# Batch 0 of an attention and gated MLP kernel: k'v partly in fp32, the first weight columns by casting loads

## The chip, the cores and the metric

The kernel runs on one core of one Trainium2 chip, in one launch. The metric is the time of one execution on the device in microseconds (us), of which the median over the runs is given.

Engines are named as in the profile: PE is TensorE (PEld its weight loads), DVE VectorE, ACT ScalarE, POOL GpSimd, SP SyncE. SP and ACT issue plain loads and stores; POOL issues the loads that convert fp32 to fp16 on the way ("casting loads").

## The reference

Linear attention without a softmax, a root-mean-square norm over each head, and a gated MLP behind it:

```python
q, k, v: (batch 8, heads 8, tokens 576, 64) fp32
kv  = einsum('bhsd,bhse->bhde', k, v)          # 64x64 per head
out = einsum('bhsd,bhde->bhse', q, kv)
x   = out / sqrt(mean(out*out, -1) + 1e-6) * g_norm
x   = x.transpose(0, 2, 1, 3).reshape(4608, 512)
ffn = (gelu(x @ w_gate) * (x @ w_val)) @ w_out  # d_ff 1536
y   = x + sigmoid(x @ w_res) * ffn              # (4608, 512) fp32
```

## The kernel before

**Tiling.** A batch has 576 tokens: 512 go through as a block of 128 partitions by NJ = 4 tokens each, and the 64 left ("the last tokens") of all batches make a ninth block at the end. For k'v all 576 tokens count, so in each batch the last 64 tokens are added to the sum. Heads go in four pairs (`pr`), because two heads of 64 fill 128 columns. The MLP's 1536 hidden columns are 12 blocks of 128 (`f`); the gate and value weights lie in four chunks of columns, of 256, 256, 512 and 512 (`WCS`), so chunk 0 is needed for blocks 0 and 1, chunk 1 for 2 and 3, and so on.

**Batch 0, "the opening".** Nothing can overlap the first batch's attention, so it is cut into pieces by pair, and these are issued in an order written out by hand: the string `opening` (L1335 to L1340). Each word is a piece, its digit the pair, and a last letter A, D or P says which engine does it (ACT, DVE, POOL). `f_piece` (L1288) turns words into instructions. Every engine works off its own instructions strictly in the order of the string. The words, in the order in which a pair needs them:

- `qc`, `kc`, `vc`: q, k, v of the pair cast from the loaded fp32 to fp16 (L1175, L1177)
- `lk`, `lv`: the last tokens of half of the heads (two pairs), cast and spread. They arrive as 32 rows of two tokens for each of four heads, row by row interleaved; `lk` multiplies k by a 0/1 column per head (`of_head`), so that a full 128-row product picks the right head (L1186), `lv` makes two copies of v (L1195)
- `qT`, `qo`: q transposed on PE, copied out of PSUM (L1203, L1206)
- `kv`: k'v of the pair in PSUM, four matmuls over the 512 tokens (L1214), two for the last tokens (L1220); `kvo`: copied out by DVE times a mask that clears the blocks between different heads (L1223)
- `o`: q (k'v) (L1228); `sq`, `rd`, `rt`, `ri`: square on ACT, sum on DVE, root on ACT, reciprocal on DVE; `t`: o times that, on DVE (L1253)
- `xT`, `xo`: t transposed on PE, copied out with a scaling by g_norm, on DVE or ACT (L1269, L1271). The fourth pair goes in two halves, a and b, from `sq` on
- `g`, `v`: the pair's share of the gate and value products of hidden blocks 0 and 1 (L1280)
- `warm`: matmuls on zeros with no use but to keep PE busy; `gelu`: the load of ACT's table for gelu
- `wcg`, `wcv`: chunk 0 of the weights cast from its fp32 load, half a chunk each (L1307); `wg`, `wv`: POOL issues the casting load of a chunk (L156)

Behind the opening PE goes on with hidden blocks 2 to 7 (`m_gval`, L443), a group for blocks 8 to 11 (L981), the residual gate (L464) and the output product (`fps`, L481), into which batch 1's attention is mixed.

**Loads.** SP issues first: q, k, v of batch 0 as fp32 (two pairs at once, then pair by pair, with the last tokens in between), then chunk 0 of both weights as fp32 in four loads (L1118). All other weights, and batch 1 from 19.5 us on, come by casting loads from POOL's queue, in the order of the opening and behind it: wg1, wv1, wg2, wv2, wg3, wv3, wr, q, k, wo, v, and so on.

Of the kernel before, what the change touches and what calls it, by code (L numbers as in the profile page):

```python
# [18 lines left out]
def kernel(  # L19
# [55 lines left out]
    pmoe, pattn = Banks(3, 1, 0, 2, opening=(0,)), Banks(4, 5, 6, 7)  # L75
# [15 lines left out]
    raw, b16_t, qr_t = {}, {}, {}  # L91
# [49 lines left out]
    wg_c, wv_c = [], []  # L141
# [58 lines left out]
    def halves(e):  # L200
        return slice(e * D, (e + 1) * D)
# [863 lines left out]

    tiles_16(0)
    raw[0, "q"] = wo_ts.bitcast(FP32)[:, 0 : H * NJ * D].rearrange("p (h x) -> p h x", h=H)
    hid_of = {}
    for which in "kv":
        if which == "k":  # L1070
            t = hidp.tile([P, NF, NJ * P], FP16, tag="hid", name=which + "f").rearrange("p a b -> p (a b)")
        else:
            t = hid_s
        hid_of[which] = t
        raw[0, which] = t.bitcast(FP32)[:, 0 : H * NJ * D].rearrange("p (h x) -> p h x", h=H)

    def load_first(which, t, lo, hi):
        nc.sync.dma_start(out=raw[0, which][:, lo:hi, :], in_=rows4(t, 0, lo, hi))


    first_raw, first_last = [], []
    for which in "kv":
        t = hid_of[which]
        rest = t[:, 2 * H * NJ * D :]
        if which == "k":
            first_last.append(rest[:, 0 : 2 * H * D].rearrange("p (j h d) -> p j h d", j=2, h=H))
        else:
            first_last.append(rest[:, 0 : 8 * D].rearrange("p (i j e d) -> p i j e d", i=2, j=2, e=2))
        first_raw.append([th_all[:, 2 * len(first_raw) + i, 0 : 2 * D] for i in range(2)])

    def load_first_last(half):
        hs = slice(half * HH, (half + 1) * HH)
        for i, t in enumerate((k, v)):
            nc.sync.dma_start(
                out=first_raw[i][half],
                in_=t[0, hs, M0:S, :].rearrange("h (p j) d -> p h (j d)", j=2),
            )

    grow = consts.tile([1, D], FP32, name="grow")
# [5 lines left out]
    for pr in range(NP // 2, NP):  # L1105
# [2 lines left out]
        if pr == NP // 2:  # L1108
            load_first_last(1)
        load_first("v", v, 2 * pr, 2 * pr + 2)  # L1110
    w_raw = {}
    for n, t in (("g", moe_w_gate), ("v", moe_w_val)):
        pool, tag = (stage, "qraw") if n == "g" else (qkvp, "k16")
        w_raw[n] = pool.tile([P, H, NJ * D], FP16, tag=tag, name=f"w{n}f")
        w_raw[n] = w_raw[n].rearrange("p a b -> p (a b)").bitcast(FP32).rearrange("p (c f) -> p c f", c=NP)
    for cs in (slice(0, NP // 2), slice(NP // 2, NP)):
        for n, t in (("g", moe_w_gate), ("v", moe_w_val)):
            nc.sync.dma_start(  # L1118
                out=w_raw[n][:, cs, :], in_=t[:, 0 : WCS[0]].rearrange("(cc p) f -> p cc f", p=P)[:, cs, :]
            )  # L1120
    ident32 = moep.tile([P, P], FP32, tag="ge", name="ident32")
    make_identity(nc, ident32)

# [11 lines left out]
    nc.vector.memset(one32, 1.0)  # L1135
    ident = consts.tile([P, P], FP16, name="ident")
    nc.vector.tensor_copy(out=ident, in_=ident32)
    of_head = consts.tile([P, HH], FP32, name="of_head")
    nc.vector.tensor_reduce(
        out=of_head, in_=ident32.rearrange("p (r h) -> p h r", h=HH), op=ALU.add, axis=mybir.AxisListType.X  # L1140
    )
    grow32 = moep.tile([1, 2, D], FP32, tag="ge", name="grow32")
    nc.vector.tensor_copy(out=grow32, in_=grow[:, None, :].to_broadcast([1, 2, D]))
    grow16 = moep.tile([1, H, D], FP16, tag="ge", name="grow16")
# [15 lines left out]
    xT0, t0 = xT_t[0], t_t[0]  # L1160
    rms0 = consts.tile([P, NJ, H], FP32, name="rms0")
    rinv0 = consts.tile([P, NJ, H], FP32, name="rinv0")
    first = {}

    tiles = {}
    engines = {"A": nc.scalar.copy, "D": nc.vector.tensor_copy, "P": nc.gpsimd.tensor_copy}

    def of_pair(pr):
        return slice(2 * pr, 2 * pr + 2), slice(pr * P, (pr + 1) * P)

    def f_cast(which, pr, copy):
        hs, _ = of_pair(pr)
        dst, src = b16_t[0, which], raw[0, which]
        if which == "v":
            copy(out=dst[:, hs, :], in_=src[:, hs, :])  # L1175
        else:
            copy(  # L1177
                out=dst.rearrange("p j h d -> p h j d")[:, hs, :, :],
                in_=src.rearrange("p h (j d) -> p h j d", j=NJ)[:, hs, :, :],
            )  # L1180

    def f_k_last(half, engs):

        raw_ = first_raw[0][half].rearrange("p (j d) -> p j d", j=2)
        for j, eng in enumerate(engs):
            eng.tensor_tensor(  # L1186
                out=first_last[0][:, j, half * HH : (half + 1) * HH, :],
                in0=raw_[:, j, None, :].to_broadcast([P, HH, D]),
                in1=of_head[:, :, None].to_broadcast([P, HH, D]),
                op=ALU.mult,  # L1190
            )

    def f_v_last(half, copy):
        raw_ = first_raw[1][half].rearrange("p (j d) -> p j d", j=2)
        copy(out=first_last[1][:, half], in_=raw_[:, :, None, :].to_broadcast([P, 2, 2, D]))  # L1195

    BANK = {"qT": (6, 4, 7, 7), "kv": (7, 5, 6, 4), "o": (2, 1, 6, 4), "xT": (7, 5, 7, 4), "xTb": (0, 0, 0, 5)}

    def f_qT(pr):
# [5 lines left out]
    def f_qT_out(pr, copy):  # L1205
        copy(out=s0["qT"][:, :, pr, :], in_=first["qT", pr])  # L1206

    def f_kv(pr):

        first["kv", pr] = ps = pattn.tile([P, P], FP32, name="kvp", bank=BANK["kv"][pr])  # L1210
        k16 = b16_t[0, "k"].rearrange("p j h d -> p j (h d)")
        hs, cs = of_pair(pr)
        for j in range(NJ):
            nc.tensor.matmul(  # L1214
                ps, lhsT=k16[:, j, cs], rhs=b16_t[0, "v"][:, hs, j * D : (j + 1) * D], start=(j == 0), stop=False
            )
        for j in range(2):
            kl = first_last[0][:, j].rearrange("p h d -> p (h d)")[:, cs]
            vl = first_last[1][:, pr // 2, j].rearrange("p e d -> p (e d)")
            nc.tensor.matmul(ps, lhsT=kl, rhs=vl, start=False, stop=(j == 1))  # L1220

    def f_kv_out(pr):
        nc.vector.tensor_tensor(out=s0["kv2"][:, pr, :], in0=first["kv", pr], in1=mask, op=ALU.mult)  # L1223
# [64 lines left out]
    def f_piece(word):  # L1288

        name = word.rstrip("0123abADP")  # L1290
        rest = word[len(name) :]
        pr = int(rest[0])
        j0, j1 = {"a": (0, NJ // 2), "b": (NJ // 2, NJ)}.get(rest[1:2], (0, NJ))
        eng = rest[-1:]
        if name in ("qc", "kc", "vc"):
            f_cast(name[0], pr, engines[eng])
        elif name == "lk":
            f_k_last(pr, (nc.gpsimd if eng == "P" else nc.vector, nc.vector))
        elif name == "lv":
            f_v_last(pr, engines[eng])  # L1300
        elif name == "warm":
            keep_warm(pr)
        elif name in ("wg", "wv"):
            (load_wg if name == "wg" else load_wv)(pr, {"a": 0, "b": 1}.get(rest[1:2]))
        elif name in ("wcg", "wcv"):
            cs = slice(2 * pr, 2 * pr + 2)
            engines[eng](out=(wg_c if name == "wcg" else wv_c)[0][:, cs, :], in_=w_raw[name[-1]][:, cs, :])  # L1307
        elif name == "qo":
            f_qT_out(pr, engines[eng])
        elif name in ("qT", "kv", "kvo", "o", "rt", "ri"):  # L1310
            {"qT": f_qT, "kv": f_kv, "kvo": f_kv_out, "o": f_o, "rt": f_sqrt, "ri": f_rinv}[name](pr)
        elif name in ("sq", "rd", "t", "xT"):
            {"sq": f_sq, "rd": f_red, "t": f_t, "xT": f_xT}[name](pr, j0, j1)
        elif name == "xo":
            f_xT_out(pr, j0, j1, eng)
        elif name == "g":
            f_mm(wg_c, 0, pr, j0, j1)
        elif name == "v":
            f_mm(wv_c, 1, pr, j0, j1)
# [3 lines left out]
    gcol = consts.tile([P, 1], FP32, name="gcol")  # L1323
    g16 = consts.tile([P, C], FP16, name="g16")
# [8 lines left out]
    keep_warm(4)  # L1333

    opening = """  # L1335
    qc0A qc1D g16 qT1 qT0 kc0A kc1D lk0P qo1A qo0D lv0P warm3 vc1D gcol vc0P kv1 qc2A kv0 kvo1 o1 kvo0 kc2P qT2 o0
    lk1D sq1 lv1P warm3 sq0 rd1 vc2P rd0 rt1 kv2 qc3P qo2A warm2 ri1 kvo2 rt0 wg1 t1 kc3A o2 qT3 sq2 ri0 xT1 warm2 vc3P t0
    qo3A wv1 rd2 kv3 wcg0A xT0 warm1 kvo3 rt2 xo1D wcv0P o3 xo0A ri2 g1 t2 wg2 sq3b v1 sq3a rd3b wcg1A xT2 wv2a rd3a g0 xo2D
    rt3 v0 wv2b wcv1A ri3 g2 t3b wg3 t3a xT3b v2 xo3bD xT3a wv3 g3b xo3aD gelu v3b g3a v3a
    """  # L1340
    pattn.turn = [6, 7, 5, 4]

# [167 lines left out]
    for blk in GROUPS:  # L1510
        t = token_sums(blk, nc.vector)
# [49 lines left out]
    for blk in range(B + 1):  # L1561
# [130 lines left out]
```

## Time and profile before

| | us |
|---|---|
| median of three runs | 320.05 |
| the three runs | 327.7, 319.15, 320.05 |
| the profiled execution, its own time | 318.52 |
| its span, first to last instruction | 316.5 |
| mean granted TensorE clock in it | 0.995 of full |
| PE / DVE / ACT / POOL busy | 308.2 / 275.7 / 217.0 / 187.4 |

The page of the profile gives busy time for each engine, and the same in 40 slices of the span (7.9 us each, a digit for tenths). A line of the timeline has start and duration in us, the engine, the line of the program, the operation, the output and its inputs with their shapes, and how many instructions are merged in it. A line on DMA issues has target and source, the queue, how many, their size as they land, and the us from issue to landing. Windows give the busy time of each engine, the DMA engines' share and GB/s of each stretch.

### The profile page before, as it was taken

What the parts mean: (1) busy time and instruction counts of PE and PEld (TensorE: products, weight loads), DVE (VectorE), ACT (ScalarE), POOL (GpSimd) and SP (SyncE); (2) the same over time, 40 slices, a digit from 0 to 9 for tenths busy, and PEclk for the clock granted to TensorE, in tenths of its full rate; (3) what the DMA queues carried; (4) which work ended last, traced back from release to release, by engine and by line L of the source; (5) the groups of instructions that cost most, each with busy time, mean ns of one, the idle gap of its engine ahead of it and who ended that gap; (6) DMA issues with size and microseconds to landing.
All of it is one profiled execution on the core that took longest, in us unless ns stands there. A gap on an engine that the chain in (4) does not pass through costs nothing.

```text
span 316.5 us, 7841 instructions
## 1 busy us (share of the span) xinstructions
PE 308.2 (97%) x3071; PEld 249.1 (79%) x3071; DVE 275.7 (87%) x489; ACT 217.0 (69%) x395; POOL 187.4 (59%) x239
## 2 busy tenths in 40 slices
PE   7899999999999999999999999999999999999993
PEld 3555756844888888888888888888888888888882
DVE  5897998989898899989998999899998777897774
ACT  4764688685958794879487948795667367736760
POOL 2883352360799579856985798408850474396332
PEclk9999999999999999999999999999999999999997
DMA  7999999899969598389936994700630003001104
GB/s 253 330 201 204 200 198 197 154 171 209 121 78 177 180 158 110 72 198 150 116 67 201 128 124 71 217 4 0 78 142 1 2 5 131 0 2 59 76 2 133
DMA packets 77398, 38.91 MB, mean 123 GB/s; under 512 B 42290, under 2 KB 75058, under 8 KB 77362
## 3 DMA queue, kind: packets, MB, share of 16 engines
q0 software_dynamic: 39296, 17.17, 43.3%
q1 hardware_dynamic: 37488, 20.71, 26.1%
q8 instruction: 24, 0.39, 0.5%
q10 hardware_dynamic: 578, 0.52, 0.5%
q14 instruction: 12, 0.10, 0.1%
HBM read 38.80 MB, written 9.44 MB: 152 GB/s over the span
## 4 chain that ended last, share of the span: by engine, by line
PE 59%; DVE 1%; issue 0%; DVEq 0%
PE Av L981 10%; PE Ag L981 10%; PE wA L549 8%; PE Fv L981 5%; PE Fg L981 5%; PE rA L600 3%; PE w L549 2%; PE Eg L981 2%; PE Ev L981 2%; PE wF L549 2%; PE wE L549 2%; PE wD L549 2%; PE rF L600 2%; PE rE L600 1%; PE kvp L218 1%; PE op L240 1%
## 5 line engine op out<-in xcount | busy, mean ns | idle before, releaser
L1018 POOL TENSOR_TENSOR hid<-ge,c 128x512 f16<-128x512 f16 x23 | 26.8, 1165 | 36.5 <-ACT ge L1012 36.5
L549 PEld LDWEIGHTS <-hid_s 128*128 128x128 f16 x384 | 37.5, 98 | 4.5
L981 PEld LDWEIGHTS <-wsv 128*128 128x128 f16 x368 | 35.6, 98 | 4.8 <-issue 0.2
L981 PEld LDWEIGHTS <-wsg 128*128 128x128 f16 x368 | 35.8, 98 | 4.2
L394 POOL TENSOR_TENSOR t<-t,g 128x512 f16<-128x512 f16 x32 | 37.8, 1210 | 0.0
L737 POOL TENSOR_TENSOR osb<-osb,t 128x512 f32<-128x512 f32 x28 | 34.0, 1244 | 0.0
L991 ACT COPY Eg<-Ag 128x512 f32<-128x512 f32 x23 | 13.4, 582 | 26.2 <-PE Ag L981 25.6
L549 PEld LDWEIGHTS <-hid 128*128 128x128 f16 x288 | 28.1, 98 | 3.3
L981 PEld LDWEIGHTS <-wg 128*128 128x128 f16 x276 | 27.0, 98 | 3.6
L981 PEld LDWEIGHTS <-wv 128*128 128x128 f16 x276 | 27.0, 98 | 3.1
L981 PE MATMUL Ag<-ts,wsg 128*128 128x256 f16 x184 | 27.6, 273 | 0.0
L981 PE MATMUL Av<-ts,wsv 128*128 128x256 f16 x184 | 27.6, 272 | 0.0
L1002 DVE TENSOR_TENSOR Fg<-Ag,d 128x512 f32<-128x512 f32 x23 | 16.0, 696 | 12.0 <-ACT d L995 9.1
L268 DVE TENSOR_REDUCE ss<-sq 128x8 f32<-128x512 f32 x32 | 20.3, 677 | 0.6 <-ACT sq L263 0.5
L549 PE MATMUL wA<-wo_ts,hid_s 128*128 128x256 f16 x168 | 20.6, 272 | 0.0
L1012 ACT ACTIVATE ge<-Eg 128x512 f16<-128x512 f32 x23 | 13.7, 597 | 9.7 <-PE Eg L981 9.7
L1012 ACT ACTIVATE ge<-c 128x512 f16<-128x512 f32 x23 | 14.4, 625 | 8.0 <-DVE c L1002 8.0
L1012 ACT ACTIVATE ge<-Fg 128x512 f16<-128x512 f32 x23 | 13.6, 591 | 8.8 <-PE Fg L981 7.0
L1002 DVE TENSOR_TENSOR c<-Ag,d 128x512 f32<-128x512 f32 x23 | 15.8, 688 | 4.2 <-PE Ag L981 4.2
L377 DVE TENSOR_TENSOR t<-op,ny 128x512 f16<-128x512 f32 x28 | 18.7, 683 | 0.9 <-POOL ny L334 0.4
L1018 DVE TENSOR_TENSOR hid<-ge,Fv 128x512 f16<-128x512 f16 x23 | 15.6, 680 | 1.5 <-ACT kv L295 1.5
L1012 ACT ACTIVATE ge<-Ag 128x512 f16<-128x512 f32 x23 | 13.7, 598 | 4.1 <-PE Ag L981 4.0
(228 smaller groups left out, 857.1 us busy)
## 6 DMA issues: line engine op xcount, KB each, us to landing
out_dram<-osb SPq DMA_DIRECT2D x14, 512.0 KB, 3.6
qraw<-in_q_dram POOLq DMA_DIRECT2D x7, 512.0 KB, 6.4
k<-in_k_dram POOLq DMA_DIRECT2D x7, 512.0 KB, 7.9
v<-in_v_dram POOLq DMA_DIRECT2D x7, 512.0 KB, 10.7
wo<-in_moe_w_out_dram POOLq DMA_DIRECT2D x3, 384.0 KB, 11.9
wg<-in_moe_w_gate_dram POOLq DMA_DIRECT2D x2, 512.0 KB, 8.4
out_dram<-osb SPq DMA_DIRECT2D x4, 256.0 KB, 5.0
wv<-in_moe_w_val_dram POOLq DMA_DIRECT2D x3, 256.0 KB, 7.5
```

The costliest lines, as they stand in the source:

```text
L218: nc.tensor.matmul(ps[halves(e), pr, :], lhsT=k16[:, h, j * D : (j + 1) * D] if j < NJ else kl[:, h, :], rhs=v16[:, h, j * D : (j + 1) * D ...
L268: nc.vector.tensor_reduce(out=out_, in_=sqs.pop((b, i)), op=ALU.add, axis=mybir.AxisListType.X)
L377: nc.vector.tensor_tensor(out=t, in0=o, in1=scale, op=ALU.mult)
L394: eng.tensor_tensor(out=t_t[blk][:, jj, :], in0=t_t[blk][:, jj, :], in1=g16, op=ALU.mult)
L549: nc.tensor.matmul(ps[:, e - es[0], :], lhsT=a[:, f, e * P : (e + 1) * P], rhs=b[:, f, :], start=(start and e == es[0] and f == 0), stop=( ...
L600: nc.tensor.matmul(out_[:, e, :], lhsT=x_[:, e, cc, :], rhs=w_[:, cc, :], start=(first and e == 0 and cc == 0), stop=(cc == 1), skip_group ...
L737: nc.gpsimd.tensor_tensor(out=res_all[of], in0=res_all[of], in1=t_t[blk][of], op=ALU.add)
L981: nc.tensor.matmul(out_[:, r, :], lhsT=lhsT, rhs=rhs, start=(first and r == 0 and c == 0), stop=(c == 1), skip_group_check=True,)
L991: nc.scalar.copy(out=tile_of("E", u), in_=ps["A", u])
L1002: nc.vector.tensor_tensor(out=dst, in0=ps["A", u], in1=sb["d", u], op=ALU.add)
L1012: nc.scalar.activation(out=ge[q], in_=source(q, "g"), func=AF.Gelu)
L1018: eng.tensor_tensor(out=dst, in0=ge[q], in1=source(q, "v"), op=ALU.mult)
```

## The change

Only batch 0 is touched.

1. The last tokens are loaded with a head's 32 rows next to one another. `lk`, `lv`, `of_head` and the spread copies go. A new word `kl` multiplies the raw fp32 rows of a head on a corner of the array (32 rows by 64 columns, placed by `tile_position`) into the pair's diagonal block, as the first part of the sum; `kv` adds the 512 tokens to it. `kl` needs two products per head, fp32.
2. The third pair (pr = 2) is not cast: its k'v over the 512 tokens is made of eight fp32 matmuls (four j, two halves of 64 columns), straight from the loaded data. `kc2` and `vc2` go.
3. Chunk 0 of both weights comes by a casting load from POOL's queue (`wg0`, `wv0`, ahead of `wg1`, `wv1`); its four fp32 loads on SP and its casts `wcg`, `wcv` go.
4. `xo2` and the second half of `xo3` move from DVE to ACT; `qc3` goes from POOL to ACT, `kc3` from ACT to POOL. The order of the string changes with it: `t1` stands before `kvo2`, `xo1D` before `kvo3`, `g0` before `v1`, and there are 8 warm matmuls instead of 11.

```diff
             nc.sync.dma_start(
                 out=first_raw[i][half],
-                in_=t[0, hs, M0:S, :].rearrange("h (p j) d -> p h (j d)", j=2),
+                in_=t[0, hs, M0:S, :].rearrange("h (p j) d -> h p (j d)", j=2),
             )
...
-    for cs in (slice(0, NP // 2), slice(NP // 2, NP)):
-        for n, t in (("g", moe_w_gate), ("v", moe_w_val)):
-            nc.sync.dma_start(
-                out=w_raw[n][:, cs, :], in_=t[:, 0 : WCS[0]].rearrange("(cc p) f -> p cc f", p=P)[:, cs, :]
-            )
...
-    of_head = consts.tile([P, HH], FP32, name="of_head")
-    nc.vector.tensor_reduce(
-        out=of_head, in_=ident32.rearrange("p (r h) -> p h r", h=HH), op=ALU.add, axis=mybir.AxisListType.X
-    )
...
+    CAST = (0, 1, 3)
...
+    def f_kl(pr):
+
+        first["kv", pr] = ps = pattn.tile([P, P], FP32, name="kvp", bank=BANK["kv"][pr])
+        for j in range(2):
+            for e in range(2):
+                rows = slice((2 * (pr % 2) + e) * (P // HH), (2 * (pr % 2) + e + 1) * (P // HH))
+                kl, vl = (first_raw[i][pr // 2][rows, j * D : (j + 1) * D] for i in range(2))
+                nc.tensor.matmul(
+                    ps[halves(e), halves(e)],
+                    lhsT=kl,
+                    rhs=vl,
+                    start=(j == 0),
+                    stop=False,
+                    skip_group_check=True,
+                    tile_position=(rows.start, e * D),
+                )
+
     def f_kv(pr):
 
-        first["kv", pr] = ps = pattn.tile([P, P], FP32, name="kvp", bank=BANK["kv"][pr])
+        ps = first["kv", pr]
...
-        for j in range(2):
-            kl = first_last[0][:, j].rearrange("p h d -> p (h d)")[:, cs]
-            vl = first_last[1][:, pr // 2, j].rearrange("p e d -> p (e d)")
-            nc.tensor.matmul(ps, lhsT=kl, rhs=vl, start=False, stop=(j == 1))
+            if pr in CAST:
...
+                continue
+            for e in range(2):
+                nc.tensor.matmul(
+                    ps[halves(e), :],
+                    lhsT=raw[0, "k"][:, 2 * pr + e, j * D : (j + 1) * D],
+                    rhs=raw[0, "v"][:, hs, j * D : (j + 1) * D],
+                    start=False,
+                    stop=(j == NJ - 1),
+                    skip_group_check=True,
+                )
...
-    qc0A qc1D g16 qT1 qT0 kc0A kc1D lk0P qo1A qo0D lv0P warm3 vc1D gcol vc0P kv1 qc2A kv0 kvo1 o1 kvo0 kc2P qT2 o0
-    lk1D sq1 lv1P warm3 sq0 rd1 vc2P rd0 rt1 kv2 qc3P qo2A warm2 ri1 kvo2 rt0 wg1 t1 kc3A o2 qT3 sq2 ri0 xT1 warm2 vc3P t0
-    qo3A wv1 rd2 kv3 wcg0A xT0 warm1 kvo3 rt2 xo1D wcv0P o3 xo0A ri2 g1 t2 wg2 sq3b v1 sq3a rd3b wcg1A xT2 wv2a rd3a g0 xo2D
-    rt3 v0 wv2b wcv1A ri3 g2 t3b wg3 t3a xT3b v2 xo3bD xT3a wv3 g3b xo3aD gelu v3b g3a v3a
+    qc0A qc1D g16 qT1 qT0 kc0A kc1D qo1A qo0D kl1 kl0 warm2 vc1D gcol vc0P kv1 qc2A kv0 kvo1 o1 kvo0 wg0 qT2 o0
+    sq1 wv0 kl2 kl3 warm2 sq0 rd1 wg1 rd0 rt1 kv2 wv1 qo2A warm1 ri1 qc3A t1 kvo2 rt0 kc3P o2 qT3 sq2 ri0 xT1 warm2 vc3P t0
+    qo3A rd2 kv3 xT0 warm1 xo1D kvo3 rt2 o3 xo0A ri2 g1 t2 wg2 sq3b g0 sq3a rd3b xT2 wv2a rd3a v1 xo2A
+    rt3 v0 wv2b ri3 g2 t3b wg3 t3a xT3b v2 xo3bD xT3a wv3 g3b xo3aA gelu v3b g3a v3a
```

More of the change, by code (lines that the diff above doesn't have):

```diff
@@ L1067 @@
     raw[0, "q"] = wo_ts.bitcast(FP32)[:, 0 : H * NJ * D].rearrange("p (h x) -> p h x", h=H)
-    hid_of = {}
     for which in "kv":
@@ L1073 @@
             t = hid_s
-        hid_of[which] = t
         raw[0, which] = t.bitcast(FP32)[:, 0 : H * NJ * D].rearrange("p (h x) -> p h x", h=H)
@@ L1078, in load_first @@
         nc.sync.dma_start(out=raw[0, which][:, lo:hi, :], in_=rows4(t, 0, lo, hi))
-    first_raw, first_last = [], []
+    first_raw = []
     for which in "kv":
[L1083 to L1088, printed above, removed]
         first_raw.append([th_all[:, 2 * len(first_raw) + i, 0 : 2 * D] for i in range(2)])
@@ L1110 @@
         load_first("v", v, 2 * pr, 2 * pr + 2)
-    w_raw = {}
-    for n, t in (("g", moe_w_gate), ("v", moe_w_val)):
-        pool, tag = (stage, "qraw") if n == "g" else (qkvp, "k16")
-        w_raw[n] = pool.tile([P, H, NJ * D], FP16, tag=tag, name=f"w{n}f")
-        w_raw[n] = w_raw[n].rearrange("p a b -> p (a b)").bitcast(FP32).rearrange("p (c f) -> p c f", c=NP)
-    for cs in (slice(0, NP // 2), slice(NP // 2, NP)):
-        for n, t in (("g", moe_w_gate), ("v", moe_w_val)):
-            nc.sync.dma_start(
-                out=w_raw[n][:, cs, :], in_=t[:, 0 : WCS[0]].rearrange("(cc p) f -> p cc f", p=P)[:, cs, :]
-            )
     ident32 = moep.tile([P, P], FP32, tag="ge", name="ident32")
@@ L1180, in f_cast @@
             )
[L1182 to L1195, printed above, removed]
+    CAST = (0, 1, 3)
     BANK = {"qT": (6, 4, 7, 7), "kv": (7, 5, 6, 4), "o": (2, 1, 6, 4), "xT": (7, 5, 7, 4), "xTb": (0, 0, 0, 5)}
@@ L1213, in f_kv @@
         for j in range(NJ):
-            nc.tensor.matmul(
-                ps, lhsT=k16[:, j, cs], rhs=b16_t[0, "v"][:, hs, j * D : (j + 1) * D], start=(j == 0), stop=False
-            )
-        for j in range(2):
-            kl = first_last[0][:, j].rearrange("p h d -> p (h d)")[:, cs]
-            vl = first_last[1][:, pr // 2, j].rearrange("p e d -> p (e d)")
-            nc.tensor.matmul(ps, lhsT=kl, rhs=vl, start=False, stop=(j == 1))
+            if pr in CAST:
+                nc.tensor.matmul(
+                    ps,
+                    lhsT=k16[:, j, cs],
+                    rhs=b16_t[0, "v"][:, hs, j * D : (j + 1) * D],
+                    start=False,
[4 more added lines that the diff above has]
+            for e in range(2):
+                nc.tensor.matmul(
+                    ps[halves(e), :],
+                    lhsT=raw[0, "k"][:, 2 * pr + e, j * D : (j + 1) * D],
+                    rhs=raw[0, "v"][:, hs, j * D : (j + 1) * D],
+                    start=False,
+                    stop=(j == NJ - 1),
+                    skip_group_check=True,
+                )
     def f_kv_out(pr):
@@ L1296, in f_piece @@
             f_cast(name[0], pr, engines[eng])
[L1297 to L1300, printed above, removed]
         elif name == "warm":
@@ L1304, in f_piece @@
             (load_wg if name == "wg" else load_wv)(pr, {"a": 0, "b": 1}.get(rest[1:2]))
-        elif name in ("wcg", "wcv"):
-            cs = slice(2 * pr, 2 * pr + 2)
-            engines[eng](out=(wg_c if name == "wcg" else wv_c)[0][:, cs, :], in_=w_raw[name[-1]][:, cs, :])
         elif name == "qo":
             f_qT_out(pr, engines[eng])
-        elif name in ("qT", "kv", "kvo", "o", "rt", "ri"):
-            {"qT": f_qT, "kv": f_kv, "kvo": f_kv_out, "o": f_o, "rt": f_sqrt, "ri": f_rinv}[name](pr)
+        elif name in ("qT", "kl", "kv", "kvo", "o", "rt", "ri"):
+            {"qT": f_qT, "kl": f_kl, "kv": f_kv, "kvo": f_kv_out, "o": f_o, "rt": f_sqrt, "ri": f_rinv}[name](pr)
         elif name in ("sq", "rd", "t", "xT"):
```

## The prediction

> **What bounds the kernel now.** I read the page first: shares of busy time, then the 40 slices, then the chain that ended last.
>
> ```profile
> span 316.5 us, 7841 instructions
> PE 308.2 (97%) x3071; PEld 249.1 (79%) x3071; DVE 275.7 (87%) x489; ACT 217.0 (69%) x395; POOL 187.4 (59%) x239
> PE   7899999999999999999999999999999999999993
> DMA  7999999899969598389936994700630003001104
> ```
>
> TensorE (PE) is full from the third slice (16 us) to the last, and the chain of waits is made of its matmuls. So only two things can move the end: when PE gets into its unbroken stretch, and whether anything breaks it later. The whole change lies before 19.35 us, where PE starts the first product behind the opening (hidden block 2). The stake is therefore a part of 19 us: it can't come near 2% (6.4 us), about what a measurement of this kernel tells from no change.
>
> Next the timeline of VectorE (DVE) in the opening:
>
> ```profile
> 9.78 1.22 DVE L1186 TENSOR_TENSOR kf<-th,of_head 128x256 f16<-128x256 f32 x2
> 10.93 1.27 DVE L1239 TENSOR_REDUCE ss<-sq 128x8 f32<-128x512 f32 x2
> 12.12 0.19 DVE L1249 RECIPROCAL rinv<-rms 128x8 f32<-128x8 f32 x1
> 12.23 0.23 DVE L1223 TENSOR_TENSOR t<-kvp,mask 128x128 f16<-128x128 f32 x1
> 12.38 0.68 DVE L1253 TENSOR_TENSOR t<-op,rinv 128x512 f16<-128x512 f32 x1
> 13.81 0.68 DVE L1239 TENSOR_REDUCE ss<-sq 128x8 f32<-128x512 f32 x1
> 16.48 0.47 DVE L1269 TENSOR_SCALAR xT<-xtp,gcol 128x512 f16<-128x512 f16 x1
> 17.17 0.76 DVE L1253 TENSOR_TENSOR t<-op,rinv 128x256 f16<-128x256 f32 x2
> ```
>
> DVE has practically no idle time from 9.78 to 18: its order of work sets the opening. The last t (t3b) starts at 17.17; transposes, scalings and the last four products follow, and PE is through 2.18 us later, at 19.35.
>
> Last the transfers. I asked for the DMA issues in narrow windows, one each, and for PE around 40 us. The three issues below were made at 22.26, 27.49 and 30.02 us.
>
> ```profile
> wo<-in_moe_w_out_dram POOLq DMA_DIRECT2D x1, 384.0 KB, 18.0
> vl<-in_v_dram POOLq DMA_DIRECT2D x1, 64.0 KB, 15.7
> wo<-in_moe_w_out_dram POOLq DMA_DIRECT2D x1, 128.0 KB, 13.9
> ```
>
> ```profile
> 39.33 1.06 PE L197 MATMUL qtp<-ident,q 128*128 128x128 f16 x16
> 40.31 2.76 PE L481 MATMUL fps<-wo,hid 128*128 128x512 f16 x12
> 43.24 0.22 PE L218 MATMUL kvp<-vl,kl 128*64 128x64 f16 x2
> 43.92 0.59 PE L481 MATMUL fps<-wo,hid 128*128 128x512 f16 x2
> ```
>
> They land at 40.26, 43.19 and 43.92; their first uses start at 40.31, 43.24 and 43.92. So the stream, busy without a gap from 2.5 us, delivers exactly in time: two of these starts come about 0.1 us late (16 transposes at 0.056 us from 39.33 end at 40.22), 0.2 us together. A PE that comes earlier waits here; one that comes 0.2 us later loses nothing.
>
> **What the Trainium skill says.** FP8 and Floating Point Precision (TensorE Precision Notes): a true fp32 product makes four passes through the array. The trace shows one fp32 matmul only, the gain column, as two weight loads and two matmuls; its moving side has one column, so no run here shows the rate. TensorE: Matmul & The Clock Gate (Part 3, row/col tiling): matmuls on different row or column groups run side by side. The trace agrees for column halves: eight kvp matmuls of 64 columns start within some 0.15 us, against 0.21 one after the other. TensorEngine Tiling (Key Properties): a change of tiling mode drains the array. The fps matmul above agrees: it starts 0.2 us after the last kvp started. DMA: Bandwidth & Descriptors (Queues, rings and completion order): an engine takes turns between the queue rows it has work for. The trace hardly shows it: the first casting load is issued at 12.07, and its packets begin near 14.6, as the fp32 queue runs dry.
>
> **The change part by part**, in the profiled execution.
>
> *Loads.* Removed: four SP loads, 1.05 MB as fp32, at 0.35 MB/us (the windows 9 to 14 us) 3.0 us. Added: two casting loads, 0.52 MB as it lands, at 0.20 MB/us (the windows from 16 us on) 2.6 us. The stream ends 0.4 us earlier. The new wg0 and wv0 are issued on POOL in front of wg1 and wv1, about 0.8 us each, from 8.95; POOL has given up kc2, vc2, qc3, lk0, lv0, lv1 and one weight cast (some 4.4 us) for kc3 alone (0.6), so both wg1 and wv1 are issued by 12.2 instead of 14.4. By the 2.5 us from issue to packets, wg0 begins at 11.5, when 0.2 MB of the fp32 queue is left (0.6 us). v3 lands at 13.0 to 13.6; I take 13.3. Its cast (0.64 us) and kv3 are done by 14.4, before DVE asks for them. wv0 is in near 15, and v1 asks for it after 16. The new layout of the last tokens keeps 512-byte rows; I cost it at nothing.
>
> *Last tokens.* kl1 and kl0 run near 6.5 to 7.5, where PE only warms up: free. kv1 and kv0 lose two matmuls each, and kvo1, kvo0, o1, o0 and sq come 0.1 us earlier. On DVE, lk1D (1.22 us) goes, but the reduction behind it waits for sq1, so it starts at 10.38 instead of 10.93: of 1.22 us, 0.55 count. Two reductions, ri1 and t1 follow, and DVE comes to kvo2 at 12.35. of_head (0.36 us at 1.9) goes from a time when DVE waits for data anyway: nothing.
>
> *kv2 in fp32.* Four 128x512 matmuls take 0.865 us on PE, so 0.42 ns a column. Estimate: four passes over 128 columns are 0.216 us. kv2 has eight of these (4 j by 2 halves): 0.86 us if the column halves run in pairs, 1.73 if not. kl2 and kl3 have eight of 64 columns: 0.43 us in pairs, 0.86 singly (0.22 with four corners at once). In order on PE: o0 issued by 10.2; kl2 and kl3 with a drain of 0.2 to 10.85; two warm matmuls (0.43) to 11.3; kv2 with a drain to 12.35. With the products one by one it is 13.65. v2 (10.70) is in by then. I take pairs, since the trace shows column halves overlapping: kvo2 runs until K = 12.7, against 12.46 before.
>
> *Behind kvo2.* Before, t1 lay between kvo2 and rd2 and covered o2 and sq2; now t1 is done, and only ri0 and t0 (0.8 us) are there. o2 and sq2 need, as before, 1.15 us from K, so rd2 starts at K+1.2 = 13.9 after a wait of 0.4. Then rd2, xo1D, kvo3, ri2, t2 and rd3b, rd3a by the durations of before: 0.66+0.45+0.26+0.17+0.66+0.74, to K+4.15. On ScalarE rt3 now stands behind xo2A, which needs the transpose of t2 and takes 0.67 us: rt3 ends near K+4.75, ri3 takes 0.18, t3b starts at K+4.95 = 17.65. That is 0.5 us later than 17.17. So DVE's relief is spent: two thirds of it had no work to put forward, and the rest goes into the wait for rd2 and into rt3.
>
> *xo2A, xo3aA.* DVE is spared 0.47 and 0.35 us; ScalarE, which lost a k cast and three weight casts for one q cast, has room. But the gelu table load (1.28 us) now follows xo3aA: 19.2 to 20.5, first gelu done at 21.1. PE needs that bank for block 3 at 19.85+1.73 = 21.6. So 0.5 us of cover; later than that, each us counts.
>
> *Sum.* Opening +0.5; of this the 0.2 us of late data near 40 to 43 us are won back, as the stream is 0.4 earlier and PE 0.5 later: +0.3. 318.52 + 0.3 = 318.8 for the profiled execution (its span of 316.5 and 2.0 around it). The runs shown have a median of 320.05, and the two close ones are 319.15 and 320.05; with the profiled one they average 319.24. So the forecast is 319.24 + 0.3 = 319.5.
>
> **Rivals.** *A, the above*, no change: 0.55.
>
> *B, the relief gets through*, 0.27. For it: DVE is full before and loses 2.0 us of work; if kv2 is ready before 12.2 and four corners overlap, and xo2A isn't late, the 0.55 us gained at rd1 reach PE. Against it: wo, vl and wo again have no slack, so the gain is at most the stream's 0.4 and about 0.1 of late starts: 318.8.
>
> *C, slower: the fp32 products run one by one.* Place: kv2 on PE, in front of kvo2, behind which DVE stands with ri0, t0 and all the rest. From the moment at which kv2 ends after 12.35 each us goes through to t3b. At 13.65 K is 14.0: +1.8 in the opening, less 0.2, +1.6: 320.8, half a percent. For it: two instructions per fp32 product, and weights of 64 columns whose load may not hide. Against it: the overlap of kvp. 0.14.
>
> *D, the clock or the supply*, 0.04: fewer warm matmuls (8 instead of 11) let the clock drop for a few us, or weights come late in a row: over 2%, 0.02. Against it: the clock is 1.00 in every window of the opening.
>
> **How the numbers follow.** A, B and C all lie within 2%: 0.96. Over 2% faster has no mechanism, 0.02 for a set of runs that differs for itself; slower 0.02. The range takes B less 0.8 and C plus 1.0 for the scatter of the runs (319.15 to 320.05 around 319.24): 318.0 to 321.8; for A alone 318.6 to 320.4.
>
> **What would show it.** kv2's matmuls end at 12.4 (A) or past 13.5 (C); kvo2 at 12.4; a gap of 0.4 on DVE ahead of rd2; t3b at 17.65 (A), under 17.0 (B), near 19 (C); block 2 at 19.85 (A), 18.9 (B), 21 (C). fps at 40.5 with no late start in A; in B at 39.9, bound to the landing. If block 2 starts earlier than 19.35 and fps with it, the DVE steps are wrong; if fps starts earlier than 39.8, the stream's 0.4 is wrong.

## The result and the profile after

| | before | after |
|---|---|---|
| median, us | 320.05 | 322.74 |
| range of the runs | 318.6 to 327.7 | 322.25 to 323.13 |
| profiled execution: own time / span | 318.52 / 316.5 | 322.25 / 320.4 |
| first v cast (pairs 0 and 1) starts | 8.02 | 9.36 |
| hidden block 2 starts | 19.35 | 23.71 |
| fps starts | 40.31 | 44.58 |
| mean granted clock | 0.995 | 0.987 |

The change makes the kernel slower: ratio 1.0099, 95% interval [1.0069, 1.0128], about 3.2 us. The run of 327.7 us was in a slow state of the chip and is left out of this ratio, so it isn't the quotient of the two medians. The forecast was 319.5 with a range up to 321.8.

From the 40 slices of the kernel before, the granted clock; from the page of the kernel after, the span and the rows of PE and of the granted clock:

```profile
PEclk9999999999999999999999999999999999999997
```

```profile
span 320.4 us, 7893 instructions
PE   5989999999999999999999999999999999999993
PEclk9599999999999999999999999999999999999999
```

The first thing to see is a 5 in the second slice of the clock row (8 to 16 us): the clock is near half of full there. The row before has no such dip. The PE row, at 9 from the third slice on, looks as it did; the loss is in the first three slices (up to 24 us).

The chain of waits up to block 2, in order of time (start, duration, what):

```profile
2.55 5.69 DMA th<-in_v_dram
8.38 0.72 PE kvp L1179 x16
...
12.94 0.65 PE kvp L1179 x16
...
14.55 1.38 PE kvp L1206 x16
```

The chain now starts with a transfer: a load of 64 KB, the last tokens of v for pairs 0 and 1, holds it for 5.69 us; the two such loads of v took 4.0 us from issue to landing (median) in the kernel before. The timeline of PE gives the same in detail:

```profile
8.38 0.72 PE L1179 MATMUL kvp<-th 32*64 32x64 f32 x16 [2.46 <-DMA th<-in_v_dram]
9.03 1.03 PE L1132 MATMUL idle<-zeros 128*128 128x512 f16 x2
14.48 1.43 PE L1206 MATMUL kvp<-hid_s,kf 128*64 128x128 f32 x16
23.71 1.03 PE L443 MATMUL gps<-xT,wg 128*128 128x512 f16 x4
43.69 1.06 PE L197 MATMUL qtp<-ident,q 128*128 128x128 f16 x16
44.58 2.75 PE L481 MATMUL fps<-wo,hid 128*128 128x512 f16 x12
47.41 0.20 PE L218 MATMUL kvp<-vl,kl 128*64 128x64 f16 x2
```

PE stands idle for 2.46 us in front of `kl1` (the line at 8.38), waiting for that load. Behind the gap two 128x512 matmuls take 1.03 us; at full clock they took 0.59 in the kernel before. The transposes from 43.69 and fps from 44.58 now follow each other without a late start.

The transfers themselves are seen in windows of half a microsecond (busy time of the engines, then granted clock, share of the 16 DMA engines, GB/s). First the kernel before, then the kernel after:

```profile
8.50:9.00 0.50, 0.49 (x7) 0.42 (x8) 0.02 (x1) 0.22 (x1) 0.42 (x1) 1.00 1.17 336
9.00:9.50 0.50, 0.50 (x9) 0.44 (x8) 0.29 (x1) 0.40 (x1) 0.00 (x0) 1.00 1.10 321
```

```profile
8.50:9.00 0.50, 0.50 (x16) 0.41 (x16) 0.00 (x0) 0.00 (x0) 0.00 (x0) 0.50 0.43 152
9.00:9.50 0.50, 0.50 (x6) 0.13 (x2) 0.14 (x1) 0.00 (x0) 0.11 (x1) 0.50 0.70 162
```

The share falls from 1.17 to 0.43 and the rate from 336 to 152 GB/s in the first of them. The loads of batch 0 have the same bytes and all of them are wanted; yet for a while the DMA engines are busy for less than half of their time.

### The profile page after: what moved, and what is told of

The parts are those of the page before. It is cut to its first block, busy times and chain, and to the rows that moved or that the text cites. A ratio compares the mean times of both kernels' runs of the same rounds, so it can differ in the third digit from the quotient of the medians.

```text
span 320.4 us, 7893 instructions
## 1 busy us (share of the span) xinstructions
PE 310.6 (97%) x3104; PEld 251.0 (78%) x3104; DVE 272.5 (85%) x483; ACT 216.6 (68%) x394; POOL 184.9 (58%) x235
## 4 chain that ended last, share of the span: by engine, by line
PE 94%; DMA 2%; DVE 1%; ACT 1%; SPq 1%; issue 0%; DVEq 0%
PE Ag L981 13%; PE Av L981 13%; PE wA L549 12%; PE Fv L981 6%; PE Fg L981 6%; PE rA L600 4%; PE gps L443 4%; PE vps L443 4%; PE fps L481 3%; PE Eg L981 3%; PE Ev L981 3%; PE wF L549 3%; PE wE L549 3%; PE wD L549 3%; PE w L549 2%; PE rps L464 2%
```

## The experiments

Theory after reading this: the last tokens' new load order is slow in itself and delays everything queued behind it on SP; the gap that it opens on PE costs the clock too. The Trainium skill, DMA: Bandwidth & Descriptors ("Why a DMA increments its semaphore by 16 and not by 1", the paragraph on how many engines), says what I had overlooked: a load rides on the largest number of the 16 DMA engines that divides the slowest dimension of both of its access patterns. `p h (j d)` has 32 rows outermost, hence 16 engines; `h p (j d)` has 4 heads outermost, hence 4. Rivals: the fp32 products (C of the prediction), the clock alone (D), the casting loads of chunk 0, or the order of rows in memory without regard to engines.

### One part alone, and all but that part

**e1**: the kernel before, with only the load order changed (and `of_head`, the 0/1 column that picks the rows, to match).

```diff
-                in_=t[0, hs, M0:S, :].rearrange("h (p j) d -> p h (j d)", j=2),
+                in_=t[0, hs, M0:S, :].rearrange("h (p j) d -> h p (j d)", j=2),
```

> The kernel before, with nothing changed but the order in which the four loads of the last tokens walk (head by head instead of row by row; of_head follows the new place of the rows). Theory 1 (a load that walks head by head is served by few of the 16 DMA engines, and all that is queued behind it on these comes late): the last tokens' v lands near 8.2 us instead of 6.5, v of the first two pairs near 9.4 instead of 8.0, the later loads some 2 us late, and the time is 2 to 4 us above before. Theory 2 (the opening's new order and the fp32 products cost it): within 0.5 us of before. Theory 3 (the clock that drops when PE idles and warms less): within 1 us of before, since the warm matmuls are all there.

322.91 us against 319.55, ratio 1.0111 [1.0069, 1.0153]. One line, no fp32 product, no casting load, and the whole loss is there. The first v cast and PE's first product in the kernel before, then in e1:

```profile
8.02 0.43 DVE L1175 CAST v<-hid_s 128x512 f16<-128x512 f32 x1 [0.81 <-DMA hid_s<-in_v_dram]
8.51 0.40 PE L1214 MATMUL kvp<-v,k 128*128 128x128 f16 x4 [1.10 <-DVE gcol L1331]
```

```profile
9.61 0.43 DVE L1175 CAST v<-hid_s 128x512 f16<-128x512 f32 x1 [1.61 <-DMA hid_s<-in_v_dram]
10.10 0.61 PE L1214 MATMUL kvp<-v,k 128*128 128x128 f16 x4 [2.64 <-DVE gcol L1331]
```

The v cast comes at 9.61 instead of 8.02. PE's gap grows from 1.10 to 2.64 us, and the product behind it takes 0.61 where it took 0.40: the late load brings the clock's loss with it, so the 3.4 us hold both.

**e6**: the counterpart: parts 2 to 4 of the change (third pair in fp32, casting loads, the moves and the new order) with the last tokens as before (`lk`, `lv`, `of_head` kept; `kv2` multiplies their copies).

> The kernel before, with all of the change but its first part: the last tokens are loaded row by row and spread by lk and lv as before; the third pair's k'v in fp32, chunk 0 of the weights by casting loads, xo2 and the end of xo3 on ACT, order of the string as in after. Theory 1: no late data, so within 1 us of before; as lk1D is back in DVE's row, the relief is gone and fp32 kv2 remains, so block 2 starts 0.5 to 1.2 us later than 19.35 and the time is 319.8 to 320.5. Theory 2: 321 or more.

319.42 us over 22 runs against 319.03, ratio 1.0009 [0.9996, 1.0022]: 0.3 us, not separated from nothing, and below the band that was expected. So parts 2 to 4 alone are nearly neutral, and without the new load order the loss is gone. What e6 doesn't test: it has no `kl`, and keeps ten warm matmuls where the kernel after has eight. (The profiled execution, at 320.45, is the longest of the 22: PE had a gap of 1.71 us before its first product and half clock from about 9.3 to 12.8 us. It doesn't stand for the median.)

**e12**: the dose. e1 with each load cut into two of two heads: the same bytes and rows, 2 heads outermost, eight loads for four.

```diff
-                out=first_raw[i][half],
-                in_=t[0, hs, M0:S, :].rearrange("h (p j) d -> h p (j d)", j=2),
+                out=first_raw[i][half][e * (P // 2) : (e + 1) * (P // 2), :],
+                in_=t[0, h : h + 2, M0:S, :].rearrange("h (p j) d -> h p (j d)", j=2),
```

> The kernel before with the last tokens loaded head by head, as in the run with only the load order changed (322.9 us), but each load cut into two of two heads (32 KB each, 8 loads for 4). Theory engines: a load's slowest dimension sets how many DMA engines carry it, so each half's 128 KB now lies on 2 engines, 64 KB on each where it was 32; at some 22 GB/s per engine (350 GB/s over 16) that is 3 us more for each half instead of 1.5, everything behind on those engines comes later by as much again, and the time is 324.5 to 327. Rival, the order of the rows in memory or the walk by heads in itself is slow, whatever the number of engines: the packets are the same, the four added issues cost at most 0.3 us, 322.7 to 323.2.

325.36 us against 319.19, ratio 1.0194 [1.0177, 1.0212], inside the band of the engine theory and outside that of its rival. The windows of this run show the engines counted:

```profile
9.50:10.00 0.50, 0.00 (x0) 0.00 (x0) 0.00 (x0) 0.00 (x0) 0.17 (x1) 1.00 1.04 342
10.50:11.00 0.50, 0.00 (x0) 0.00 (x0) 0.00 (x0) 0.00 (x0) 0.00 (x0) 0.50 0.14 45
11.50:12.00 0.50, 0.45 (x5) 0.46 (x6) 0.06 (x1) 0.20 (x1) 0.46 (x1) 0.50 0.13 44
```

A share of 0.13 to 0.14 is two engines of sixteen (0.125), and 44 GB/s is two sixteenths of 350, the rate before. While the last-token loads finish, the other fourteen have nothing to move, and SP doesn't get the next loads out: its second pair of v loads takes 2.72 us to issue (8.54 to 11.26), the first pair took 1.05. With 32 rows outermost the loss is nothing, with 4 heads 3.4 us, with 2 heads 6.2 us. An estimate from these rates gives most of it: the four loads of e1 (eight here) are 256 KB; at 22 KB/us (half of 44 GB/s) an engine needs 0.7 us for its share of sixteen, 2.9 for its share of four, 5.8 for its share of two, so 2.2 and 5.1 us more. The step from four engines to two comes out at 2.9 against the measured 2.8; both sums fall 1.1 to 1.2 short, and the clock may be the rest, which isn't shown. The count of four is less clear in the windows than that of two: in e1 the share touches 0.26 at 82 GB/s for 0.1 us (8.9 to 9.0), in the kernel after it stays at 0.40 or above.

### The clock

**e3** was meant to put twelve warm matmuls before `kl1`. The digits of a word are read one at a time, so the kernel had one more, not twelve.

> The kernel after, with twelve more warm matmuls ahead of kl1, to fill PE's idle time from 5.9 to 8.4 us while it waits for the last tokens. Theory 1: the clock stays at 1.00 but the data are as late as in after, so block 2 moves by less than 0.7 us and the time is within 0.7 us of after. Theory 3: PE's chain from 8.4 to 16 us runs at twice the speed, block 2 starts 2 us earlier or more, and the time falls by 2 to 3 us. Theory 2: between the two, by 0 to 1 us.

322.67 us, 1.0111 [1.0073, 1.0148], as the kernel after; PE still waits 2.59 us, so it says nothing on the clock. **e9** repeats it with the twelve:

```diff
-    ... qo1A qo0D kl1 kl0 warm2 ...
+    ... qo1A qo0D warm3 warm3 warm3 warm3 kl1 kl0 warm2 ...
```

> The kernel after, with twelve warm matmuls (2.6 us at full clock) ahead of kl1, so that PE has work from 5.9 to about 8.5 us while it waits for the last tokens (in e3 only one was added, as the digits of the word were read singly). Clock theory (the idle PE loses its clock and runs its chain from 8.4 to 15.9 us at half speed, and that is most of the loss): block 2 starts 1.5 us or more earlier than 23.71, the time is 320 to 321.2. Lateness theory (the data behind the slow loads are 1.3 to 2.5 us late whatever PE does): block 2 at 22.5 or later, the time at 321.8 or more.

322.08 us against 319.3, 1.0077 [1.0049, 1.0105]. PE's timeline:

```profile
6.43 2.75 PE L1132 MATMUL idle<-zeros 128*128 128x512 f16 x12
9.12 0.47 PE L1179 MATMUL kvp<-th 32*64 32x64 f32 x16
12.70 0.48 PE L1179 MATMUL kvp<-th 32*64 32x64 f32 x16 [0.72 <-DMA th<-in_v_dram]
13.64 1.09 PE L1206 MATMUL kvp<-hid_s,kf 128*64 128x128 f32 x16
22.54 1.03 PE L443 MATMUL gps<-xT,wg 128*128 128x512 f16 x4
```

The clock stays up, `kl1` with `kl0` take 0.47 instead of 0.72 and `kv2` 1.09 instead of 1.43. Most of the loss is still there: `kl2` waits for the second of the v loads until 12.70, and block 2 starts at 22.54 instead of 23.71. Time and block 2 lie in the band of the lateness theory. Filling the gap alone thus gives back some 0.7 us of 3.2, by the medians; the intervals of e9 and of the kernel after overlap. (The twelve run on until `kl1` at 9.12, 0.74 us later than in the kernel after, so a shorter filling may give more.) The Trainium skill, TensorE: Matmul & The Clock Gate (Part 1, the clock gate), gives an idle window of about 3.4 us after which the clock is halved; here the clock fell behind a gap of 2.46 us.

**e11**: the clock by itself: the kernel before without its first three warm matmuls.

```diff
-    qc0A qc1D g16 qT1 qT0 kc0A kc1D lk0P qo1A qo0D lv0P warm3 vc1D ...
+    qc0A qc1D g16 qT1 qT0 kc0A kc1D lk0P qo1A qo0D lv0P vc1D ...
```

> The kernel before without the three warm matmuls ahead of vc1D, so that PE idles from 6.4 to 7.0 and from 7.1 to 8.5 us, with all data in time. Clock theory: PE falls to half clock near 8.5 us and runs its chain to about 13 us at half speed, the time is 0.8 to 2.5 us above before. Lateness theory: within 0.3 us of before.

320.03 us over 22 runs against 319.3, 1.0014 [0.9998, 1.003]: 0.45 us by the ratio, not separated from nothing, and between the bands of the two theories. Block 2 comes at 20.93 in its profiled execution of 320.74. Behind a gap of 1.37 us the warm matmuls in its trace run at half speed, while the window over them has the granted clock at full:

```profile
11.24 1.06 PE L1154 MATMUL idle<-zeros 128*128 128x512 f16 x2
```

```profile
10.00:12.00 2.00, 2.00 (x15) 1.42 (x13) 1.74 (x4) 1.12 (x3) 1.78 (x4) 1.00 1.09 346
```

So a granted clock of 1.00 doesn't show a fast array; the duration of a known matmul does.

### Other layouts, with the rest of the change

**e5**: the kernel after, but the last tokens lie one token to a row, 64 rows, so that 64 is outermost (16 engines), and `kl` is one product per head over 64 rows.

```diff
-                out=first_raw[i][half],
-                in_=t[0, hs, M0:S, :].rearrange("h (p j) d -> h p (j d)", j=2),
+                out=first_raw[i][half].rearrange("p (h d) -> p h d", h=HH),
+                in_=t[0, hs, M0:S, :].rearrange("h s d -> s h d"),
```

> The kernel after, with the last tokens loaded token by token: 64 partitions of four heads by 64, still four loads on SP in the same places, now walking 64 tokens outermost; kl is then one fp32 product of 64 rows for each head. Theory 1 (only the walk head by head is slow): v of the first two pairs lands near 8.0 to 8.4 us, the clock stays full, block 2 starts at 19.4 to 20.3 us, as the sum of the prediction has it, and the time is 319 to 320.3. Theory 2 (new order and fp32 products cost the rest): block 2 starts past 21 us and the time stays above 321.

321.67 us, 1.0077 [1.0057, 1.0096]: by the ratios a fifth of the loss is gone, within the intervals of the two. That is against the theory that only the walk by heads is slow, which asked for 319 to 320.3. Two variants of it ask what else could hold it: **e7** casts the third pair instead of multiplying it in fp32 (`kc2P`, `vc2P` back, 2 added to `CAST`); **e8** loads chunk 0 as fp32 and casts it, as before.

> As e5, but the third pair's k and v are cast on POOL again and its k'v is four fp16 matmuls. If fp32 kv2 costs what the prediction said (1.05 us on PE against 0.5, and kvo2 0.25 us later), the time is within 0.3 us of e5, a little below or above as POOL's casts delay wv0 and wg1; if fp32 kv2 was the larger part (one by one, 1.7 us), it is 0.8 us or more below e5.

> As e5, but chunk 0 of both weights is loaded as fp32 on SP and cast on ACT and POOL as in before. The stream of transfers then ends 0.4 us later (3.0 us for 1.05 MB of fp32 against 2.6 for the casting loads). If the opening sets the time, it is the same as e5 within 0.3 us; if the stream near 40 us does, 0.4 us above e5.

e7: 321.14 us, 1.0072 [1.0057, 1.0087]; e8: 321.95, 1.0095 [1.0078, 1.0112]. Neither differs from e5 beyond the intervals. By the medians the fp32 third pair costs 0.5 us (0.2 by the ratios), and the casting loads save 0.3; neither is separated from nothing. e8 also brings a loss of its own: in its trace the opening keeps its clock, but PE waits 0.98 us, until 20.99, for a weight cast on ACT. What the layout alone leaves of the loss shows on PE in e7's trace:

```profile
7.67 0.45 PE L1178 MATMUL kvp<-th 64*64 64x64 f32 x8 [1.16 <-DMA th<-in_v_dram]
12.26 1.04 PE L1132 MATMUL idle<-zeros 128*128 128x512 f16 x2
```

`kl1` still waits for its load, 1.16 us in place of 2.46, and the granted clock is 0.50 from 10 to 16 us.

**e10**: e5 with five warm matmuls ahead of `kl1`.

```diff
-    ... qo1A qo0D kl1 kl0 warm2 ...
+    ... qo1A qo0D warm3 warm2 kl1 kl0 warm2 ...
```

> As e5 (last tokens loaded token by token, on all engines), with five warm matmuls ahead of kl1 to fill 6.7 to 7.7 us. Clock theory: PE stays at full clock, kvo2 near 13 us, block 2 at 19.6 to 20.5, the time at 318.8 to 319.8, so equal to before or a little better. Lateness theory: within 0.5 us of e5, 321.2 to 322.

320.18 us over 22 runs, 1.0021 [1.0007, 1.0036]; the interval is clear of that of e5, though the time lies between the bands of the two theories. With sixteen engines and no gap, the layout without the spread copies is 0.7 us slower than the kernel before, no longer 3.2. Its timeline, PE and DVE:

```profile
6.45 1.24 PE L1132 MATMUL idle<-zeros 128*128 128x512 f16 x5
7.62 0.45 PE L1178 MATMUL kvp<-th 64*64 64x64 f32 x8
11.52 0.45 PE L1178 MATMUL kvp<-th 64*64 64x64 f32 x8 [0.68 <-DMA th<-in_v_dram]
12.43 1.09 PE L1205 MATMUL kvp<-hid_s,kf 128*64 128x128 f32 x16
21.33 1.03 PE L443 MATMUL gps<-xT,wg 128*128 128x512 f16 x4
```

```profile
8.52 0.43 DVE L1153 CAST v<-hid_s 128x512 f16<-128x512 f32 x1 [1.41 <-DMA hid_s<-in_v_dram]
18.72 0.20 DVE L1241 RECIPROCAL rinv<-rms 128x8 f32<-128x8 f32 x1 [0.77 <-ACT rms L1237]
19.02 0.76 DVE L1245 TENSOR_TENSOR t<-op,rinv 128x256 f16<-128x256 f32 x2
```

The v cast still comes 0.5 later than before, and `kl2` waits 0.68 for its v rows, now of 256 bytes. Few engines aren't the reason here: from 6 to 7 us the DMA share is 1.12, but the rate 199 GB/s, where the kernel before moves 346 to 350. Whether it is the row size wasn't separated.

Put side by side, as us above the kernel before by the ratios, the runs say more than one by one:

| | gap in front of `kl1` | gap filled |
|---|---|---|
| 4 heads outermost | 3.2 (kernel after) | 2.5 (e9) |
| 64 tokens outermost | 2.5 (e5) | 0.7 (e10) |

Either repair alone gives back some 0.7 us, which the intervals don't separate from nothing; both together give back 2.5. Late data and a slow array lie over each other in the same stretch, and the one that is left still holds the end, so neither can be given a share of the 3.2. (This reading fits the four runs; the lower row also has other rows in memory and half as many `kl` products.)

### Attempts to keep the layout and use all engines

A load of one head has 32 rows outermost. Five runs cut the loads by head or moved them to other queues.

**e2**: sixteen loads of one head, over the queues of ACT, POOL and SP. **e4**: the four loads of the kernel after, issued by POOL instead of SP.

```diff
+            queue = ((nc.scalar, nc.gpsimd), (nc.gpsimd, nc.sync))[half][i]
+            for h in range(HH):
+                queue.dma_start(
+                    out=first_raw[i][half][h * (P // HH) : (h + 1) * (P // HH), :],
+                    in_=t[0, half * HH + h, M0:S, :].rearrange("(p j) d -> p (j d)", j=2),
+                )
```

> The kernel after, with the last tokens loaded by one transfer for each head (32 rows each, sixteen small loads instead of four, spread over the ACT, POOL and SP queues), the same rows in the same places. Theory 1: the slow landing is gone, PE starts kl near 6.5 us, block 2 starts near 19.4 to 19.9 us as in the sum of the prediction, and the time is 318.5 to 320 us, within 0.5 us of before. Theory 2: block 2 still starts 2 us or more after 19.35, and the time stays above 321. Theory 3: the clock is full again since PE doesn't idle for 2.5 us, so it can't be told from theory 1 here.

> The kernel after, with the four loads of the last tokens issued by POOL instead of SP, same order head by head, still fp32. Theory 1, if POOL's queue spreads such a load over all engines: packets and landing as in before, time within 0.7 us of before. Theory 1, if POOL's queue also uses few engines: they no longer stand in SP's queue, but take turns with it on the same engines, so the time lies between before and after, near 321. Theory 2: no gain beyond 0.5 us over after.

e2: 323.74 us, 1.0126 [1.0084, 1.0168]. e4: 322.86, 1.01 [1.0061, 1.014]. Neither gains, and both miss what the theory of the engines asked for. In e2 the first v cast came at 8.28, so the data were in early again; but POOL's eight issues (4.2 us) stood ahead of the identity matrix, and q's transposes began late, at 9.01 instead of 5.31. In e4 they began at 7.76 for the same reason, and the first v cast came at 9.67. **e13**, **e14** and **e15** avoid that: e13 gives the first half's loads by head to ACT and leaves the second on SP; e14 gives the first half to ACT and the second to POOL, behind the identity; e15 is e14 with two warm matmuls ahead of `kl1`.

> The changed kernel, its first two last-token loads (pairs 0 and 1) cut into one load per head with 32 rows outermost, issued by ScalarE's queue instead of SP's, eight issues ahead of its first cast; the other two loads as in the changed kernel. Theory engines: all 16 engines carry the first half, so k0 and v0 no longer wait for the 4 that are filled first; v0's first cast near 8.3 instead of 9.4, half of the loss is gone unless the second half's loads, still on 4 engines, decide: 320.8 to 321.8. Rival, small loads in the changed layout are slow whoever carries them: no earlier v0, 322.5 to 323.2.

> The changed kernel with all its last-token loads cut into one load per head (32 rows outermost, 16 KB): pairs 0 and 1 by ScalarE's queue, pairs 2 and 3 by GpSimd's after the identity matrix is made, none by SP. Theory engines: the loads are spread over all engines, v0's first cast near 8.2, v3 lands near 13; with the array's clock still lost to the earlier and longer gap, 319.8 to 321.0. Rival, slow rows or queues that share badly: 322.3 or more.

> The run before with two matmuls of 128x512 ahead of the first corner products, so that TensorE does not idle before them. Theory engines plus clock: the forecast of the prediction comes back, 319.0 to 320.2, at or below the kernel before; block 2 near 19.8. Rival, data late for another reason: no better than 321.

All three missed, and on the wrong side: 325.52 us, 1.0191 [1.0166, 1.0216]; 324.67, 1.0168 [1.0147, 1.0188]; 324.81, 1.0175 [1.0152, 1.0197]. e14 and e15 lie in the bands of their rivals (slow rows or queues that share badly; data late for another reason), e13 above both of its bands. The timeline of issues and casts of e14:

```profile
1.78 0.51 SPq L1076 DMA_DIRECT2D hid_s<-in_v_dram  x1
6.81 0.37 SPq L1076 DMA_DIRECT2D wo_ts<-in_q_dram  x1
```

```profile
1.33 1.78 ACTq L1086 DMA_DIRECT2D th<-in_k_dram  x4
5.07 2.25 ACTq L1086 DMA_DIRECT2D th<-in_v_dram  x4
7.36 0.62 ACT L1155 CAST q<-wo_ts 128x512 f16<-128x512 f32 x1 [5.35 <-DMA th<-in_k_dram]
```

ACT issues four loads and then nothing until 5.07; its cast of q, at 4.81 in the kernel after, stands behind the issues and begins at 7.36. SP's fourth load goes out at 6.81 instead of 3.68. With four loads on ACT's queue (e2) that load of SP went out at 4.62, and with POOL's loads alone beside SP's (e4) at 2.34, so the delay goes with the loads on ACT; what held the two queues, the trace doesn't say. The four runs that split the load show that this costs more than it gives here. They neither support nor refute the count of engines, since each of them also moved the first issues, the identity matrix or ACT's casts; slow small loads, as a rival, stay open.

No run found a version that beats the kernel before; e6 equals it.

## Why the prediction was wrong

**The step that failed** is the sentence "The new layout of the last tokens keeps 512-byte rows; I cost it at nothing." The rows do keep their size, but the slowest dimension went from 32 to 4 and with it the load from sixteen engines to four. e1 sizes the term: 3.4 us, against my nought, with the clock lost in the longer gap counted in. I had looked at bytes and packets and not at how a load is spread. The prediction had a page's sentence on how an engine takes turns, and not the one on how many engines carry a load.

**What hung on it.** "kl1 and kl0 run near 6.5 to 7.5, where PE only warms up: free": `kl1` began at 8.38, behind a wait of 2.46 us. This step fails by itself too. With sixteen engines `kl1` still began at 7.67, behind a wait of 1.16 us (e7), and filling that place is worth 1.8 us (e10 against e5, by the ratios). "v2 (10.70) is in by then": v2's load was issued at 6.82 instead of 6.11 and landed 6.4 us later, at 13.2. "The clock is 1.00 in every window" spoke of a PE whose gap was 1.10 us. Rival D had the clock right as a mechanism, with a chance of 0.04. Its cause, fewer warm matmuls, is a part of it: before, three stood ahead of the first product that waits for a load; after, two are left there, and they stand behind `kl1`. The rest is the late load, which made the gap longer.

**What held.**
- The sum of +0.3 without the load's price: e6, which has parts 2 to 4 only, shows +0.3 (1.0009). As `kl` isn't in it, the agreement is partly luck.
- fp32 in pairs, A against C: `kv2` was put at 0.86 us in pairs (1.05 with the drain) and 1.73 singly. With the clock up it takes 1.03 us to the next matmul (12.43 to 13.46 in e10). C's singly isn't seen. `kl2` with `kl3`, 0.43 in pairs or 0.65 with the drain, take 0.41 (12.70 to 13.11 in e9). That also fits four corners at once with a drain (0.22 and 0.2); the two aren't separated. The line that was read as a drain can't show one: the fps matmul at 43.92 starts as its weights land.
- Behind `kvo2`: t3b was put at K+4.95. K, the end of `kvo2`, is 13.86 in e10 and t3b starts at 19.02, K+5.16. In the kernel after K is 16.25 and t3b comes at 21.41, K+5.16 again. The sequence was right to 0.2 us; K itself was 12.7 in the forecast and came 3.55 late. The wait of ri3 for rt3 behind `xo2A` is there, 0.77 us.
- The place of the give-back: block 2 is 4.36 later, fps 4.27, the vl product 4.17. The 0.2 us of late starts near 40 us are gone, as foreseen.
- Chunk 0 by casting loads: 0.4 us earlier in the forecast, 0.3 by e8 against e5, within the noise.

**The size of the give-back stays open.** Against the profiled execution of before (318.52), the kernel after is 3.73 longer with block 2 4.36 later, e10 1.21 with 1.98, e6's execution 1.93 with 2.50: 0.6 to 0.8 us won back behind block 2. But e9, the same program behind the opening, is 3.03 longer with 3.19, e4 2.66 with 2.97, and e1, without parts 2 to 4, 3.24 with 3.10: 0.2, 0.3 and nothing. These are single executions, and the forecast's 0.2 lies within their scatter. e6's +0.3 is thus the forecast's sum but perhaps not its two terms: no trace of a median run of e6 shows where block 2 starts.

So the claim that the stake is "a part of 19 us" and that the start of block 2 counts held to within 0.8 us. What was wrong was a load's price, and the taking of a product that waits for it as free.

## What to carry to other kernels

When a diff reorders a DMA's dimensions, read the outermost dimension of both sides first: its size decides how many engines carry the load, and an equal number of bytes and packets says nothing about that. A small load on few engines delays not only its own reader but what is queued behind it (here v of pairs 0 and 1, 6.2 us from issue to landing instead of 4.9); look for windows in which the DMA share drops while loads are still waiting. When two delays lie over each other, repair both before you price either. Put a number on every edit that "keeps" something, with its worst case, for the range; a term of nought has no range.

## What the runs showed of the hardware that I had not expected

- Loads of 32 KB with two heads outermost held the rate of the whole stream near 44 GB/s for some 2.5 us (10.5 to 13.0 us in e12), 0.13 to 0.15 of the DMA engines' time.
- A gap of 2.46 us on PE in the opening was followed by half clock until about 15 us, one of 1.71 (e6) until 12.8, one of 1.16 (e7) from about 9.6 to 16.5. One of 1.10 us, with three warm matmuls ahead of it, was not, nor one of 0.79 in e8. The runs give no length of gap that is safe.
- Half-speed matmuls (two of 128x512 in 1.06 us instead of 0.59) stand under a granted clock of 1.00 in e11.
- With eight loads on ACT's queue and eight on POOL's beside SP's, SP's fourth load went out at 6.81 us (e14); in the kernel after, by SP alone, nine loads were out by then.
